# Two more triangular inverses on GpSimd, a weight preparation at another rank, and a planner with transfer lanes and re-measured durations

## The chip, the cores and the metric

The kernel runs on one core of a Trainium2 chip. The metric is the device time of one execution in microseconds (us). The core has five engines that run side by side, each with its own stream of instructions in a fixed order: TensorE (PE; its weight loads are PEld), VectorE (DVE), ScalarE (ACT), GpSimd (POOL) and SyncE (SP), which issues the DMA transfers. An instruction waits on semaphores until its inputs are there, and what stands behind it on its engine waits too.

## The reference

Three parts run one after the other: a recurrence over 768 steps for 4 batches of 8 heads, whose state is a 40x40 matrix for each head, and two feed-forward layers on the 3072 resulting rows of 320 values, with 2048 inner values each.

```
B, H, S, D = 4, 8, 768, 40
for t in range(S):
    y[:, :, t] = einsum('bhd,bhde->bhe', rt, state)
    Sa = einsum('bhde,bhe->bhd', state, at)
    state = state * wt[..., None, :] - einsum('bhd,bhe->bhde', Sa, bt) + einsum('bhd,bhe->bhde', vt, kt)
x = y.transpose(0, 2, 1, 3).reshape(B * S, H * D)
h = x @ w_in;  g = h * tanh(log1p(exp(h)));  x = g @ w_out      # layer 1
h = x @ w_in2; g = h * cos(h);               out = g @ w_out2    # layer 2
```

## The kernel before

The 32 heads are split into two halves of 16, and the 768 steps into 24 chunks of 32. A chunk of one half has a number g from 0 to 47, the two halves in turn; two successive numbers make a pair, bt = g // 2. Inside a chunk the recurrence is solved in closed form, for which a triangular 32x32 matrix must be inverted for every head. For each chunk these functions run:

- `pre(g)` prepares it. On VectorE: a running product of the decays (L571), its reciprocal (L576), a reverse scan (L577), and multiplies that make the operands AM (L585, two) and the keys KB (L591, two); on GpSimd two memsets of AM (L599). On TensorE the products between steps (L608, 8 matmuls for each bank, evicted in four pieces on VectorE, L618) and the transposed keys (L641). The part to be inverted is stored to DRAM (L631, L632).
- `inverse(bt)` loads both chunks of a pair into XM (L668), one matrix on each of 64 partitions, and inverts 16x16 blocks in 14 rounds of a multiply (L683) and an add (L681), then a memset of the diagonal (L690). Result stored (L694), loaded again in another layout as TT (L698). These 28 steps and the memset run on one engine: `own` says whether that is GpSimd or VectorE.
- `halves(bt)` joins the blocks to the 32x32 inverse: a transpose (L725) and one operation (L728) on VectorE, 32 small matmuls each of L720 and L722, a copy on ScalarE (L396).
- `chain(g)` is the recurrence proper. TensorE: L791, the product with the inverse (L805), L837, L863, L889, L933; VectorE: FR (L873), the next chunk's SV (L900), Y (L908). FR is loaded by L742 and L743, and the result is stored by L952.

Layer 1 runs on blocks of 256 rows: XR is loaded, ScalarE rounds it to XH (L1050), VectorE takes the rest XL (L1052), TensorE multiplies both with the split weights (h, L993), then the activation (L1066 to L1071) and the second product (o, L974). The first block needs the first four chunks of both halves. Layer 2 is like it (L1008, L1025), in blocks of 512. The weights are split into two parts by `prep`: ScalarE L465, VectorE L470 and L475, and a subtraction on GpSimd (L505). `prep` for layer 1 starts with the kernel, so it shares the engines with the first chunks.

Nothing of the order is left to a compiler. Every step is a `Task` with an engine, a duration, predecessors, and slots in rings of buffers (7 for PE, AM and FL, 3 for TT, 4 PSUM banks). `Plan.run` simulates the five engines with these numbers and always takes the task that can start first, by rank and priority (`prio`, lower is earlier); instructions are emitted in that order. TensorE's tasks have a column count (`cols`): where the count in a tick is under HOT, the planner doubles durations, and above DENSE it may keep matmuls of one tile shape together. A transfer is an SP task with a fixed latency, and it asks SP_SAFE us of spare time of a ring's buffer. Lines of `inverse` that the change touches:

```
own = bt >= 3
IE = G if own else V
t = P.add("POOL" if own else "DVE", 0.1 + 0.0022 * i * (15 - i) if own else 0.165, step(i, add), ...)
```

Of the kernel before, what the change touches and what calls it, by code (L numbers as in the profile page):

```python
# [20 lines left out]
S = 768  # L21
# [34 lines left out]
class Task:  # L56
    __slots__ = ("eng", "dur", "fn", "preds", "acq", "rel", "aset", "lat", "prio", "end", "n_wait", "succ", "ready", "cols", "engs", "takes", "name", "durs", "bias", "ffn", "port", "mode", "soft", "pull", "mate")

    def __init__(self, eng, dur, fn, preds=(), acq=(), rel=(), aset=None, lat=None, prio=0.0, cols=0.0, bias=BIAS, port=False):
# [16 lines left out]
        self.mate = None  # L76

# [3 lines left out]
DENSE = 4400.0  # L81
HOT = 2750.0
# [6 lines left out]
SP_SAFE = 1.0  # L89
# [9 lines left out]
class Plan:  # L99
# [23 lines left out]
    def run(self):  # L123
# [15 lines left out]
        tick, hot, count, tick_no = TICK, False, 0.0, 0  # L139
        order = {id(t): i for i, t in enumerate(self.tasks)}  # L140
        while done < len(self.tasks):
# [67 lines left out]
            if e == "PE":  # L209
# [20 lines left out]
            t.end = free[e] + (0.2 if t.lat is None else t.lat)  # L230
# [6 lines left out]
            for u in t.succ:  # L237
                for x in u.engs:
                    u.ready[x] = max(u.ready[x], free[e] + (HOP.get((e, x), 0.15) if t.lat is None else t.lat))
# [12 lines left out]
def body(ctx, tc, ins, out):  # L252
# [147 lines left out]
    def pa(key):  # L400
        return bank[P.at(key)]
# [22 lines left out]
    am_on, GLE = lambda g, d: ("DVE", 0.385), ("DVE",)  # L424
# [14 lines left out]
    def prep(layer, names, prio, after, stage, stage2, half):  # L439
# [5 lines left out]
        for kind, k, c0, n in jobs(layer):  # L445
# [32 lines left out]
            t3 = P.add("DVE", dve(n, 0.5), cvt1, preds=[t1], prio=prio, port=True)  # L478
# [75 lines left out]
    def pre(g):  # L554
# [38 lines left out]
        t_k = fifo("kb", P.add(*am_on(g, 0.65), kb_f(0), preds=[t_rp], acq=[("KB", k("KB"))], prio=pr, port=True))  # L593
        t_b = P.add(*am_on(g, 0.65), kb_f(1), preds=[t_k, t_a1], rel=[k("RP")] + ([] if g == 1 else [k("IN")]), prio=pr, port=True)
# [6 lines left out]
        t_z0 = P.add("POOL", 0.31, az_f(0), preds=[t_a1], prio=pr)  # L601
        t_z1 = P.add("POOL", 0.31, az_f(1), preds=[t_z0], prio=pr)
# [8 lines left out]
        t_g = P.add("PE", 0.46, g1, preds=[t_z1, t_b], acq=[("PA", k("G"), 4)], cols=925, prio=pr)  # L611
# [11 lines left out]
        for c2 in range(2):  # L623
            for p in range(2):
                t_gl.append(P.add("DVE", 0.27, gev(p, c2), preds=[t_g], rel=[k("G")], prio=pr))
# [17 lines left out]
        def kbe(e):  # L643
            def f(eng):
                kp = pa(k("KT"))[64 * e:64 * e + 64, 0:4 * QP].rearrange("r (q x) -> r q x", x=QP)
                for p in range(2):
# [4 lines left out]
                    cols=500, prio=pr)  # L651
        KBe[g] = [P.add(KBE, 0.4 + 0.2 * e, kbe(e), preds=[t_t], rel=[k("KT")], prio=pr) for e in range(2)]

    def inverse(bt):
# [17 lines left out]
        own = bt >= 3  # L672
# [684 lines left out]
```

## Time and profile before

| what | value |
|---|---|
| device time, median of 3 runs | 1081.68 us (1081.59 to 1082.09) |
| profiled execution, span from first to last instruction | 1089.5 us |
| TensorE busy in it | 1006.6 us (92%) |
| VectorE busy | 742.0 us (68%) |
| ScalarE busy | 544.0 us (50%) |
| GpSimd busy | 429.8 us (39%) |

The profiled execution is one execution with the hardware's recorder on, and its span is 7.8 us longer than the median of the timed runs. Durations are read from it, differences are applied to the median. An engine's busy time counts only its computing instructions. The clock column of the profile gives the TensorE clock that the chip granted, 1.00 being full speed.

### The profile page before, as it was taken

The page shows a single profiled execution, that of the slowest core. Times are in us where ns is not written, and L with a number is a line of the kernel's source. Part 1 is how long each engine was busy: PE and PEld are TensorE (multiplying, and loading weights), DVE is VectorE, ACT ScalarE, POOL GpSimd, SP SyncE. Part 2 cuts the span into 40 slices and gives each one's busy share as a digit, 9 for nine tenths or more (in the row PEclk, how much of TensorE's full clock was granted, in tenths as well). Part 3 has the DMA queues.
Part 4 walks back from the last instruction along what each step waited for, and adds up shares of the span by engine and source line. Part 5 has one row for each costly group of instructions (what it writes and reads, how often), then busy time and mean ns, then how long its engine had stood idle before and what let it go on. Part 6 is the DMA issues. An engine that isn't in the chain of part 4 may idle for free.

```text
span 1089.5 us, 36321 instructions
## 1 busy us (share of the span) xinstructions
PE 1006.6 (92%) x14888; PEld 926.8 (85%) x14888; DVE 742.0 (68%) x1652; ACT 544.0 (50%) x1338; POOL 429.8 (39%) x883
## 2 busy tenths in 40 slices
PE   1276899999999999999999999999999999999998
PEld 1265789888889988888998999999999999999997
DVE  8999888787577786678643797446655656565555
ACT  2345875655474655656564544434433434343433
POOL 4217646547344554355420242103333333333332
PEclk9999999999899999999999999999999999999999
DMA  6547665556445565455533543211100202010100
GB/s 206 149 134 231 173 166 145 154 143 170 108 137 160 145 168 127 122 152 151 137 90 100 173 152 96 85 42 35 42 13 1 54 1 54 1 40 1 25 1 25
DMA packets 109078, 111.88 MB, mean 103 GB/s; under 512 B 64112, under 2 KB 88688, under 8 KB 108912
## 3 DMA queue, kind: packets, MB, share of 16 engines
q1 hardware_dynamic: 108592, 109.24, 36.6%
q8 instruction: 117, 1.92, 0.7%
q14 instruction: 49, 0.40, 0.1%
q10 hardware_dynamic: 320, 0.33, 0.1%
HBM read 91.43 MB, written 18.09 MB: 101 GB/s over the span
## 4 chain that ended last, share of the span: by engine, by line
PE 75%; DVE 12%; DMA 5%; issue 4%; ACT 2%; SPq 1%; POOL 1%; DVEq 0%; POOLq 0%; ACTq 0%
PE bank L993 17%; PE bank L974 15%; PE bank L1008 14%; PE bank L1025 13%; PE bank L889 3%; PE bank L608 2%; DVE SV L900 2%; PE bank L863 1%; DMA VR<-in_vR_dram 1%; PE bank L641 1%; PE bank L837 1%; PE bank L791 1%; PE bank L933 1%; PE bank L805 1%; DVE AM L618 1%
## 5 line engine op out<-in xcount | busy, mean ns | idle before, releaser
L1154 POOL TENSOR_TENSOR GL<-H,GH 128x512 fp32r<-128x512 f32 x94 | 121.9, 1298 | 235.7 <-ACT GH L1152 219.1
L683 POOL TENSOR_TENSOR XT<-XM 64x14 f32<-64x14 f32 (+6 forms) x294 | 97.0, 330 | 174.5 <-DMA XM<-l_d 153.7
L396 ACT ACTIVATE FL<-bank 64x160 f32<-64x160 f32 (+1 forms) x375 | 101.4, 295 | 104.5 <-PE bank L641 51.6
L1145 ACT ACTIVATE T<-T,half_pi 128x512 f32<-128x512 f32 x96 | 69.5, 723 | 105.3 <-DVE T L1142 105.3
L1138 DVE TENSOR_SCALAR T<-bank 128x512 f32<-128x512 f32 x96 | 66.4, 692 | 76.7 <-PE bank L1008 63.2
L681 POOL TENSOR_TENSOR XM<-XM,XT 64x14 f32<-64x14 f32 (+6 forms) x294 | 106.0, 360 | 22.3
L1071 DVE TENSOR_TENSOR GL<-H,GH 128x512 fp32r<-128x512 f32 x96 | 70.1, 734 | 65.5 <-ACT GH L1068 63.7
L1147 DVE TENSOR_TENSOR H<-bank,T 128x512 f32<-128x512 f32 x96 | 66.1, 689 | 54.1 <-ACT T L1145 54.1
L1066 ACT ACTIVATE H<-bank 128x512 f32<-128x512 f32 x96 | 57.5, 598 | 87.9 <-PE bank L993 87.0
L1152 ACT ACTIVATE GH<-H 128x512 fp32r<-128x512 f32 x96 | 60.7, 632 | 73.9 <-DVE H L1147 73.9
L993 PE MATMUL bank<-XH,wih 128*128 128x256 f32 x448 | 95.4, 295 | 0.2 <-ACT GH L1068 0.2
L993 PE MATMUL bank<-XH,wil 128*128 128x256 f32 x448 | 89.7, 282 | 0.0
L993 PE MATMUL bank<-XL,wih 128*128 128x256 f32 x448 | 89.5, 282 | 0.0
L608 PE MATMUL bank<-AM,KB 104*64 104x64 f32 x768 | 37.0, 246 | 48.9 <-DVE KB L591 46.8
L618 DVE TENSOR_TENSOR AM<-bank,maskG 64x128 f32<-64x128 f32 x192 | 55.4, 288 | 35.8 <-PE bank L608 26.8
L608 PEld LDWEIGHTS bank<-AM,KB 104*64 104x64 f32 x768 | 30.5, 155 | 53.4 <-issue 35.4
L993 PEld LDWEIGHTS bank<-XH,wih 128*128 128x128 f32 x448 | 70.0, 192 | 2.2 <-ACT GH L1068 0.3
L993 PEld LDWEIGHTS bank<-XL,wih 128*128 128x128 f32 x448 | 69.7, 192 | 0.0
L993 PEld LDWEIGHTS bank<-XH,wil 128*128 128x128 f32 x448 | 69.6, 192 | 0.0
L1142 DVE SCALAR_TENSOR_TENSOR T<-T,bank 128x512 f32<-128x512 f32 x96 | 65.7, 685 | 2.4
L993 PE MATMUL bank<-XH,wix 128*128 128x256 f32 x224 | 67.1, 300 | 0.0
L900 DVE TENSOR_TENSOR SV<-bank,PE 40x160 f32<-40x160 f32 x184 | 58.9, 320 | 7.0 <-PE bank L889 3.8
(179 smaller groups left out, 2931.6 us busy)
## 6 DMA issues: line engine op xcount, KB each, us to landing
VR<-in_vR_dram SPq DMA_DIRECT2D x96, 160.0 KB
IN<-in_inT_dram SPq DMA_DIRECT2D x94, 161.4 KB
FR<-in_rI_dram SPq DMA_DIRECT2D x48, 180.0 KB
FR<-in_vF_dram SPq DMA_DIRECT2D x48, 144.0 KB
RA<-in_w_in_dram SPq DMA_DIRECT2D x12, 512.0 KB
RA<-in_w_out_dram SPq DMA_DIRECT2D x10, 512.0 KB
SV<-in_vS_dram SPq DMA_DIRECT2D x96, 52.0 KB
TMP<-in_w_in_dram SPq DMA_DIRECT2D x9, 512.0 KB
```

The lines of the kernel that those rows point to most:

```text
L396: A.activation(o, i, AF.Copy)
L608: PE.matmul(gp[c0:c0 + 64, q // 2], kb()[:, q].rearrange("p a t -> p (a t)"), am()[0:104, :, q], start=True, stop=True)
L681: IE.tensor_tensor(out=b[:, 0:i, i + 1:16], in0=b[:, 0:i, i + 1:16], in1=tv, op=ALU.add)
L683: IE.tensor_tensor(out=tv, in0=bc(b[:, i:i + 1, i + 1:16], (2 * n, i, w)), in1=bc(b[:, 0:i, i:i + 1], (2 * n, i, w)), op=ALU.mult)
L900: V.tensor_tensor(out=svn[r, p, :, 64 * h:64 * h + D], in0=fp[r, :, C:], in1=bc(pev(h)[r, :, C:C + 1], (40, 4, D)), op=ALU.mult)
L974: PE.matmul(o, l[:, f, tsl], r, start=(first and f == 0 and i == 0), stop=(last and f == 1 and i == 2))
L993: PE.matmul(hp[:, f], pss[i][0], pss[i][1], start=(i == 0), stop=(i == 7))
L1008: PE.matmul(bank[P.at((key, "h"))][:, 0:512], pss[i][0], pss[i][1], start=(i == 0), stop=(i == 7))
L1025: PE.matmul(o, l, r, start=(ft == 0 and i == 0), stop=(ft == NFF - 1 and i == 2))
L1071: gl = P.add(GLE, (dve(512),), lambda eng, Hv=Hv, key=key: EN[eng].tensor_tensor(out=GL_t[P.at((key, "gl"))], in0=Hv(), in1=GH_t[P.at((key ...
L1145: c = P.add("ACT", act(512, False, 1), lambda f=f, Tv=Tv: A.activation(Tv(f), Tv(f), AF.Sin, scale=-TWO_PI, bias=half_pi), preds=[b], aset ...
L1154: gl = P.add(*((VG, (pool(512), dve(512))) if final and quad == 7 else ("POOL", pool(512))), lambda eng, f=f, Hv=Hv, key=key: EN[eng].tens ...
```

## The change

`own` becomes true from the second pair on: the inverses of the pairs bt = 1 and bt = 2 go to GpSimd too; that of bt = 0 stays on VectorE. The preparation of layer 1's weights goes from priority -4921 to -4941, so it ranks ahead of two chunks' more tasks. The rest changes the planner only: SP's transfers go through a model with eight lanes, each with its own size and latency, in place of a fixed latency; TensorE's instruction fetching is modelled in blocks of 256; durations, column counts and the two column thresholds are replaced; SP_SAFE becomes 0. No instruction but those of the two inverses changes its engine by an edit of its own. The new numbers also give every engine another order. Lines behind L134 move by 17 to 36 (L683 becomes L719, L805 becomes L841, L993 becomes L1029).

```
-SP_SAFE = 1.0
+SP_SAFE = 0.0
-DENSE = 4400.0
-HOT = 2750.0
+DENSE = 5240.0
+HOT = 3277.0
+ISSUE, GAP_I, LANES, LAND = 0.36, 0.06, 8, 0.15
+DMAS = {"pre.ld": ((0.85, 1.65), (0.75, 1.65)), "inverse.st": ((0.2, 1.1), (0.2, 1.1)),
...
+BLOCK, AHEAD_C, FETCH = 256, 78, 3.5
...
+            if t.dm:
+                cur = st
+                for size, l0 in t.dm:
+                    cur = max(cur, lanes[nd % LANES]) + ISSUE
+                    srv = max(srv, cur + l0) + size
+                    lanes[nd % LANES], nd = srv, nd + 1
+                    cur += GAP_I
+                dur = cur - st
...
+            t.end = srv + LAND if t.dm else free[e] + (0.2 if t.lat is None else t.lat)
...
-    am_on, GLE = lambda g, d: ("DVE", 0.385), ("DVE",)
+    am_on, GLE = lambda g, d: ("DVE", 0.43), ("DVE",)
...
-        own = bt >= 3
+        own = bt >= 1
...
-                t = P.add("POOL" if own else "DVE", 0.1 + 0.0022 * i * (15 - i) if own else 0.165, step(i, add), preds=[t], lat=0.1 if own else 0.04, prio=pr, port=True)
+                t = P.add("POOL" if own else "DVE", 0.1 + 0.0022 * i * (15 - i) if own else 0.22, step(i, add), preds=[t], lat=0.1 if own else 0.04, prio=pr, port=True)
...
-                t = P.add("PE", 0.48, mm, preds=list(preds) + [t], cols=880, acq=[("PH", (key, "h"))] if first else [],
+                t = P.add("PE", 0.48, mm, preds=list(preds) + [t], cols=1024, acq=[("PH", (key, "h"))] if first else [],
...
-    S_V = P.add("DVE", 2.0, setup_v, prio=-9e5)
+    S_V = P.add("DVE", 4.0, setup_v, prio=-9e5)
...
-    wr1 = prep(1, ("w_in", "w_out"), -4921.0, [W1_AFTER()], ("RW", "H"), ("RL", "RA1"), half1)
+    wr1 = prep(1, ("w_in", "w_out"), -4941.0, [W1_AFTER()], ("RW", "H"), ("RL", "RA1"), half1)
```

In the rows of the order below, a row is a line, an operation, and its output and inputs with their tile. A number behind a name tells which buffer of a ring it is; TT_233 to TT_235 are the inverses of three successive pairs in turn.

VectorE, before, where the second pair's inverse begins (XM and XT are the inverse, PE, RP, AM and KB a chunk's preparation):

```order
L576 RECIPROCAL D1R<-PE_200 104x8
L577 SCALAR_TENSOR_TENSOR RP_217<-IN_195,D1R 104x264
L585 TENSOR_TENSOR AM_207<-IN_195,PE_200 40x256
L591 TENSOR_TENSOR KB_219<-IN_195,RP_217 104x8x32
L585 TENSOR_TENSOR AM_207<-IN_195,PE_200 40x256
L683 TENSOR_TENSOR XT<-XM 64x14
L591 TENSOR_TENSOR KB_219<-IN_195,RP_217 104x8x32
L681 TENSOR_TENSOR XM<-XM,XT 64x14
L571 SCALAR_TENSOR_TENSOR PE_201<-IN_194,D_193 104x264
L683 TENSOR_TENSOR XT<-XM 64x26
L576 RECIPROCAL D1R<-PE_201 104x8
L577 SCALAR_TENSOR_TENSOR RP_217<-IN_194,D1R 104x264
```

The same chunks' preparation on VectorE in the new order:

```order
L607 SCALAR_TENSOR_TENSOR PE_200<-IN_195,D_193 104x264
L726 MEMSET XM 64x16
L511 SCALAR_TENSOR_TENSOR H_179<-TMP,H_179 128x512
L612 RECIPROCAL D1R<-PE_200 104x8
L613 SCALAR_TENSOR_TENSOR RP_217<-IN_195,D1R 104x264
L621 TENSOR_TENSOR AM_207<-IN_195,PE_200 40x256
L627 TENSOR_TENSOR KB_219<-IN_195,RP_217 104x8x32
L621 TENSOR_TENSOR AM_207<-IN_195,PE_200 40x256
L607 SCALAR_TENSOR_TENSOR PE_201<-IN_194,D_193 104x264
L627 TENSOR_TENSOR KB_219<-IN_195,RP_217 104x8x32
```

Steps of an inverse stood between the multiplies; now the memset that ends the first pair's is the last of them here, and the two chunks' preparation stands together.

TensorE, before, up to the first feed-forward matmul (L993; TT_235 is pair three's inverse, RS the right-hand sides that it is multiplied with):

```order
L720 MATMUL bank_146<-TA,TT_235 32x32 x32
L722 MATMUL bank_146<-TT_235,TB 32x16 x32
L805 MATMUL bank_145<-RS_236,TT_235 32x40 x16
L805 MATMUL bank_147<-RS_237,TT_235 32x40 x16
L837 MATMUL bank_144<-ident,ZS_232 40x128 x4
L993 MATMUL bank_148<-XH_187,wih_164 128x256 x2
```

The same place in the new order (TT_233 is pair four's inverse, L841 the product with it, L1029 the first feed-forward matmul):

```order
L644 MATMUL bank_147<-AM_206,KB_219 64x64 x8
L841 MATMUL bank_145<-RS_236,TT_233 32x40 x16
L841 MATMUL bank_144<-RS_237,TT_233 32x40 x16
L677 MATMUL bank_146<-ident,KB_219 128x104 x4
L873 MATMUL bank_147<-ident,ZS_232 40x128 x4
L644 MATMUL bank_145<-AM_207,KB_219 64x64 x8
L899 MATMUL bank_146<-VR_224 64x64 x8
L873 MATMUL bank_147<-ident,ZS_232 40x128 x4
L1029 MATMUL bank_148<-XH_187,wih_164 128x256 x2
```

The first feed-forward matmul stood behind the products with pair three's inverse; now it stands behind those with pair four's, and six more small groups follow the first of them.

GpSimd, before, ahead of its first inverse, which is pair four's (L505 is a weight subtraction, L599 the memset of AM):

```order
L599 MEMSET AM_203 64x256 x2
L505 TENSOR_TENSOR wil_165<-H_180,wih_164 128x512
L505 TENSOR_TENSOR wix_166<-H_181,wix_166 64x512
L599 MEMSET AM_204 64x256 x2
L505 TENSOR_TENSOR wol1a<-H_179,woh1a 128x512
L683 TENSOR_TENSOR XT<-XM 64x14
L681 TENSOR_TENSOR XM<-XM,XT 64x14
L683 TENSOR_TENSOR XT<-XM 64x26
```

GpSimd, in the new order, ahead of its first inverse, which is pair two's:

```order
L541 TENSOR_TENSOR wil_165<-H_180,wih_164 128x512
L541 TENSOR_TENSOR wix_166<-H_181,wix_166 64x512
L635 MEMSET AM_207 64x256 x2
L719 TENSOR_TENSOR XT<-XM 64x14
L717 TENSOR_TENSOR XM<-XM,XT 64x14
L719 TENSOR_TENSOR XT<-XM 64x26
L717 TENSOR_TENSOR XM<-XM,XT 64x2x13
```

The first inverse on GpSimd came when the memsets had gone once round AM's ring of seven (AM_203 to AM_209) and on to AM_204; now it comes in the first round, at AM_207, and ahead of the first subtraction of the second weight matrix (wol1a).

## Rows read from the trace of the kernel before

**Rows 1.** Busy by stretch: stretch, us; PE PEld DVE ACT POOL (instructions); clock, DMA, GB/s.

```profile
0.00:115.00 115.00, 55.73 (x1325) 47.24 (x1326) 105.29 (x303) 47.19 (x133) 42.84 (x102) 1.00 0.62 177
115.00:150.00 35.00, 31.06 (x750) 27.95 (x749) 30.14 (x72) 28.85 (x73) 18.05 (x39) 1.00 0.64 180
150.00:200.00 50.00, 49.06 (x929) 44.91 (x928) 41.23 (x108) 32.01 (x95) 35.94 (x87) 1.00 0.54 146
200.00:600.00 400.00, 386.19 (x8772) 351.04 (x8771) 270.86 (x715) 228.60 (x684) 176.23 (x540) 0.98 0.52 138
600.00:1089.50 489.50, 484.61 (x3121) 455.71 (x3119) 294.48 (x457) 207.35 (x356) 156.77 (x116) 1.00 0.16 46
```

**Rows 2.** TensorE's waits up to 115 us: line, releaser: us, times, longest.

```profile
PE bank L608 <- DVE KB L591: 44.4, 8, 17.0
```

**Rows 3.** Order of time around the first feed-forward matmul: start, us, engine, line, operation.

```profile
113.78 0.95 DVE L1052 TENSOR_TENSOR XL<-XR,XH 128x768 fp32r<-128x768 f32 x1
114.73 0.78 PE L993 MATMUL bank<-XH,wih 128*128 128x256 f32 x2
```

**Rows 4.** Order of time: L889 early and later, [idle before].

```profile
95.08 2.19 PE L889 MATMUL bank<-FR,FL 104*64 104x72 f32 x32
...
139.62 1.22 PE L889 MATMUL bank<-FR,FL 104*64 104x72 f32 x32 [0.96 <-DVE FR L873]
```

**Rows 5.** Lines of VectorE up to 160 us: instructions, busy us, mean ns, idle before.

```profile
L683 DVE TENSOR_TENSOR XT<-XM 64x14 f32<-64x14 f32 (+6 forms) x42 | 9.4, 224 | 0.8
L681 DVE TENSOR_TENSOR XM<-XM,XT 64x14 f32<-64x14 f32 (+6 forms) x42 | 8.1, 193 | 0.9
```

**Rows 6.** Order of time: first and last steps of pair two's and pair four's inverse.

```profile
47.93 0.17 DVE L683 TENSOR_TENSOR XT<-XM 64x14 f32<-64x14 f32 x1
...
71.82 0.07 DVE L690 MEMSET XM<- 64x16 f32 x1
...
89.90 0.21 POOL L683 TENSOR_TENSOR XT<-XM 64x14 f32<-64x14 f32 x1 [3.65 <-DMA XM<-l_d]
...
102.72 0.12 POOL L690 MEMSET XM<- 64x16 f32 x1
```

**Rows 7.** The page's costliest groups: the multiplies of the inverses on GpSimd.

```profile
L683 POOL TENSOR_TENSOR XT<-XM 64x14 f32<-64x14 f32 (+6 forms) x294 | 97.0, 330 | 174.5 <-DMA XM<-l_d 153.7
```

**Rows 8.** Lines of VectorE by form, up to 160 us: the chunks' work.

```profile
L585 DVE TENSOR_TENSOR AM<-IN,PE 40x256 f32<-40x256 f32 x28 | 17.7, 631 | 0.3
...
L900 DVE TENSOR_TENSOR SV<-bank,PE 40x160 f32<-40x160 f32 x32 | 10.3, 321 | 1.4 <-PE bank L889 0.8
...
L908 DVE TENSOR_TENSOR Y<-bank,PE 104x128 f32<-104x128 f32 x16 | 4.6, 289 | 0.3
...
L576 DVE RECIPROCAL D1R<-PE 104x8 f32<-104x8 f32 x15 | 3.0, 201 | 0.2
```

**Rows 9.** Order of time on VectorE and GpSimd, 99 to 105 us.

```profile
99.21 0.85 POOL L681 TENSOR_TENSOR XM<-XM,XT 64x36 f32<-64x36 f32 x1
...
101.86 0.41 DVE L591 TENSOR_TENSOR KB<-IN,RP 104x256 f32<-104x256 f32 x1
...
102.93 1.57 POOL L505 TENSOR_TENSOR wol1a<-H,woh1a 128x512 fp32r<-128x512 f32 x1
103.36 1.42 DVE L591 TENSOR_TENSOR KB<-IN,RP 104x256 f32<-104x256 f32 x1
```

**Rows 10.** Order of time: pair three's inverse stored, and its product.

```profile
98.65 0.95 SPq L694 DMA_DIRECT2D t_d<-XM  x2
...
112.82 1.29 PE L805 MATMUL bank<-RS,TT 32*32 32x40 f32 x64 [1.06 <-ACT TT L396]
```

**Rows 11.** Lines of TensorE by form, 200 to 560 us: the chunks' work.

```profile
L889 PE MATMUL bank<-FR,FL 104*64 104x72 f32 x1024 | 38.2, 229 | 0.0
...
L720 PE MATMUL bank<-TA,TT 16*32 16x32 f32 x1088 | 13.0, 194 | 1.6 <-DVE D1R L576 1.1 <-issue 0.5
```

**Rows 12.** TensorE's waits, 115 to 600 us, the largest one of issue.

```profile
PE bank L722 <- issue: 3.0, 4, 1.7
```

More of the change, by code (lines that the diff above doesn't have):

```diff
@@ L76, in __init__ @@
         self.mate = None
+        self.code = 64 if self.name == "chain.ztm" and dur < 0.4 else CODE.get(self.name, 8)
+        self.dm = DMAS.get(self.name) if eng == "SP" else None
+        if self.dm and "prep" in self.name and dur < 0.5:
+            self.dm = ((1.05, 1.3),)
 TIE = 97
 TICK = 10.24 / 3
-DENSE = 4400.0
-HOT = 2750.0
+DENSE = 5240.0
+HOT = 3277.0
 MODE = {"pre.g1": "128x64", "chain.rvz": "128x64", "chain.fmm.f": "128x64", "chain.rhs": "128x32",
@@ L88 @@
 WAIT = 8.0
-SP_SAFE = 1.0
+SP_SAFE = 0.0
+ISSUE, GAP_I, LANES, LAND = 0.36, 0.06, 8, 0.15
+DMAS = {"pre.ld": ((0.85, 1.65), (0.75, 1.65)), "pre.ldm": ((0.2, 1.0), (0.2, 1.0)), "inverse.ld": ((0.25, 1.2), (0.25, 1.2)),
+        "inverse.st": ((0.2, 1.1), (0.2, 1.1)), "inverse.<lambda>": ((0.5, 1.5),),
+        "load_step.f1": ((0.95, 1.65), (0.5, 1.65)), "load_step.f2": ((0.9, 1.5), (0.9, 1.5)),
+        "load_step.f3": ((0.2, 1.2), (0.2, 1.2)), "prep.<lambda>": ((2.15, 1.4),), "chain.yst": ((0.37, 1.25), (0.37, 1.25)),
+        "layer1.ld": ((0.8, 1.4), (0.25, 1.3), (0.25, 1.3)), "layer1.<lambda>": ((0.4, 1.05),),
+        "layer2.ld": ((0.3, 1.3),) * 4, "layer2.store": ((0.27, 1.3),) * 2}
+CODE = {"pre.g1": 32, "early.uu": 64, "early.<lambda>": 64, "halves.mm.f": 128, "chain.rhs": 64, "chain.zmm": 64,
+        "chain.rvz": 32, "chain.fmm.f": 32, "chain.sel": 20, "outs.mm": 6, "outs_wide.mm": 6}
+BLOCK, AHEAD_C, FETCH = 256, 78, 3.5
 def mode_cost(a, b):
@@ L225, in run @@
                     count += t.cols
-                recent.append((st + dur, t.cols))
+                at, per = st, dur / t.code
+                for i in range(code, code + t.code):
+                    if i % BLOCK == 0 and i // BLOCK in fetched:
+                        w = max(0.0, fetched[i // BLOCK] - at)
+                        at, dur = at + w, dur + w
+                        self.starved += w
+                    if (i + AHEAD_C) % BLOCK == 0:
+                        b = (i + AHEAD_C) // BLOCK + 1
+                        fetched[b] = max(at, fetched.get(b - 1, 0.0) - FETCH / 2) + FETCH
+                    at += per
+                code += t.code
+                recent.append((st + dur, t.cols))
+            if t.dm:
[6 more added lines that the diff above has]
+                dur = cur - st
             free[e] = st + dur + sw
@@ L238, in run @@
                 for x in u.engs:
-                    u.ready[x] = max(u.ready[x], free[e] + (HOP.get((e, x), 0.15) if t.lat is None else t.lat))
+                    u.ready[x] = max(u.ready[x], t.end if t.dm else free[e] + (HOP.get((e, x), 0.15) if t.lat is None else t.lat))
                 u.n_wait -= 1
@@ L878, in chain @@
         for h in range(2):
-            ve[h] = P.add("DVE", 0.41, rve(h), preds=[r0] + z[2 * h:2 * h + 2] + [ve[i] for i in range(h)], rel=[k("V")], prio=pr)
+            ve[h] = P.add("DVE", 0.43, rve(h), preds=[r0] + z[2 * h:2 * h + 2] + [ve[i] for i in range(h)], rel=[k("V")], prio=pr)
         yb, yc = divmod(c, 2)
@@ L919, in chain @@
             if not last:
-                s = [P.add("DVE", 0.315, sev(h, p), preds=[ft, io[nx][2]], prio=pr) for p in range(2)]
+                s = [P.add("DVE", 0.34, sev(h, p), preds=[ft, io[nx][2]], prio=pr) for p in range(2)]
             sevs += s
```

54 lines of the change are left out of this document (28 added, 26 removed).

## The prediction

> **What bounds the kernel now.** I read the table by stretches first, then the waits of TensorE, then the order of time around the first feed-forward matmul. TensorE is busy in 1006.6 of the 1089.5 us (the five stretches added) [rows 1]. That work is the same before and after, so what can move is its 82.9 us of idle time. 59.3 of them lie ahead of 115, 3.9 from 115 to 150, 0.9 to 200, 13.8 from 200 to 600 and 4.9 behind. So the start is the stage to read. There VectorE is busy 105.3 of 115 us, ScalarE 47, GpSimd 43, and TensorE's one large wait is for the keys that VectorE makes, 44.4 us in 8 waits, the longest 17.0 [rows 2]. VectorE works at XL from 113.78, the last input of layer 1's first block, and the first feed-forward matmul starts at 114.73 [rows 3]. From there TensorE has layer 1 to fill itself with, and it is never idle for long. The start is VectorE's, the rest is TensorE's.
>
> A second thing is lost in the start. The same 32 matmuls of L889 take 2.19 us at 95.08 and 1.22 at 139.62 [rows 4], though the granted clock reads 1.00 in both stretches [rows 1]. So what a step at the start is worth is counted at the price that it would have later, since that is where it would otherwise stand.
>
> **The inverses leave VectorE.** One inverse is 28 multiply and add steps and a memset. VectorE ran 84 of these steps, three pairs of chunks, in 9.4 + 8.1 us [rows 5], so 5.85 us a pair; two pairs leave it, **11.7 us**. The steps were strewn between other work: those of the second pair took from 47.93 to 71.82, 23.9 us, while the fourth pair's on GpSimd took from 89.90 to 102.72, 12.9 us [rows 6], with other work in between. So a step is slower on GpSimd (330 ns in the mean [rows 7] against 208) and the inverse is through sooner after its start. GpSimd has room: 42.8 us busy of 115 [rows 1], about 69 with two more inverses.
>
> **What fills VectorE instead.** The order has the same 15 weight tiles prepared ahead of XL as before, but more of the attention. Preparation of chunks gains 18 instructions of six lines (two L571, L576 and L577, four L585, two L591, four L618; L585 is the largest group at 631 ns and L576 the smallest at 201 [rows 8]), 8.1 us by their means. The recurrence gains eight L900 (321 ns, the largest group), four L873 and four L908 (289 ns, the smallest) [rows 8], 5.4 us. One transpose and one L728 add 0.9. In go 14.4, out 11.7: **+2.7 us**, and XL moves from 113.8 to 116.5. If some 3.5 of VectorE's 9.7 us of gaps [rows 1] closed as well, it would come at 113; that is the lower end.
>
> **What else the first matmul waits for.** In TensorE's order both products with the inverse of pair three stood ahead of the first feed-forward matmul (L805); now those of pair four stand there too, and pair four's inverse is the third in a row on GpSimd. Pair two can start near 44. Three inverses at 12.9, four weight subtractions among them that GpSimd did not have there before, 1.57 us at most [rows 9], and the memsets of the keys, 7.5 in all: 90 if GpSimd never waits. If pair four waits for its chunks' preparation, which stands some 74 us of work deep on VectorE, its transfer ends near 82 and its inverse at 95 (estimates, from the order and the means by line). The way from there is read from pair three: store issued at 98.65, product at 112.82 [rows 10], 14.2 us, so 104 to 109. Then come six small groups of TensorE, 7 us at the slow rate: 111 to 116. SP's queue can add to that. In the new order the store of an inverse stands behind loads of FR that wait for TensorE and VectorE, and the loads behind it wait too. One such wait of 6 us makes it 122. By VectorE the first matmul comes at 117.4, by this path at 111 to 122. I take **118**, 3.3 us later than now, nearer VectorE's row because that one is counted and the path has slack at several places.
>
> **What TensorE has done by then.** Ahead of its first feed-forward matmul the order now holds 16 more of L608, 4 of L641, 32 each of L791, L805, L720 and L722, 24 of L863, 32 of L889, 16 of L933 and 12 of L837: one pair of chunks, give or take a step. From 200 to 560 these ten lines take 187 us for 32 chunks (L889 the largest with 38.2, L720 the smallest with 13.0 [rows 11]), 11.7 a pair, and 11.0 without the overlap at the seams. That work no longer stands between 118 and the end. Gain: 11.0 - 3.3 = **7.7 us**. By the lower end (first matmul at 114) it is 11.7, by the upper (122) 3.7.
>
> **Everything else that moves.** The planner's numbers (durations, columns, eight transfers in flight, fetched instructions) emit nothing; they reorder. Behind the start I cost that at nothing, since TensorE is busy 386 of 400 us there [rows 1] with feed-forward work that can be drawn ahead of a wait. Where the cover fails the row is issue, in which nothing visible is waited for, 3.0 us in the largest of four lines and 7.6 in all [rows 12]. The new plan can win perhaps 5 of it, or lose as much, since it has 106 changes of tile shape among the small matmuls against 93. Bounds -5 and +5, taken as 0. Layer 2's order is the same but for a few neighbours.
>
> **Locks between VectorE and GpSimd.** A multiply of VectorE took 1.42 us at 103.36, and its like 0.41 at 101.86; a 1.57 us GpSimd subtraction had started at 102.93 [rows 9]. So the one engine can hold up the other. The 56 steps moved to GpSimd can each do this: from nothing to 56 x 0.33 = 18 us of VectorE, and half a step each is 9.2. I leave it at nothing in the sum: the 0.41 at 101.86 lies within the fourth pair's inverse [rows 6, 9], and the three others of its kind in there took no longer, 0.40 to 0.42. Both ends stay for the range. The Trainium skill (SBUF — State Buffer, Who interferes with whom) says that a VectorE instruction with two SBUF inputs contends with a GpSimd instruction that reads SBUF, and that the second waits for the whole of the first. By that rule the trace agrees at 103.36, and the rule speaks against this change: it is what gives the first rival its chance.
>
> **The rivals.** (a) The locks take it back: 9.2 us on top of 116.5, the first matmul at 126.6, 11.9 late, gain 11.0 - 11.9: 1082 to 1083. With locks a little shorter it is 1081. For it: VectorE stays as full and GpSimd is fuller. Against: the multiplies beside pair four's inverse did not stretch. (b) The chain of inverses sets the start, and the kernel ends **slower**. TensorE takes its instructions in order, so nothing passes a product that waits for T. If each inverse is stretched by 3 us, as single steps are beside VectorE (one took 0.85 us at 99.21 [rows 9] against the mean of 0.33), and SP holds one store for 6 us, the first matmul starts at 109 + 7 + 9 + 6 = 131, 16.3 late: 5.3 lost, 1087. It decides from 126 on, where the delay passes the 11.0. For it: the order leaves no feed-forward work ahead of the product. Against: pair four's chunks are prepared early and little else stands between the inverses. (c) The start gains as forecast and the issue waits go too: 7.7 + 5, so 1069. (d) The change does not do what it says: the new numbers fit the chip no better than the old, and behind the start the plan returns the gain in waits of TensorE from 118 to 200, where there were 4.8 us. Within 2 us of now; it shares (a)'s time.
>
> **How the numbers follow.** The profiled execution's span is 1089.5 us and the median of the runs 1081.68, 7.8 less; differences are taken from the median. 1081.68 - 7.7 = **1074**. Chances: forecast, 1070 to 1079, 0.55; (c) 0.13; (a) and (d) together 0.16; (b) 0.16. The 8-in-10 range leaves out a tenth on each side: 1065 below (gain 11.7 and the five of issue) and 1086 above, within (b). About 0.2%, 2.2 us, is what a measurement of this kernel can tell from no change. Faster takes the forecast and (c), 0.68; same is most of (a) and (d), 0.15; slower is (b) and the worst of (a), 0.17.
>
> **What would show it.** In the profile after, no XM or XT steps on VectorE behind some 45 us, and 56 more on GpSimd. The first L1029 matmul (now L993) at 116 to 121. TensorE's idle time ahead of the first one at most 62 us though it comes later. VectorE about 90% busy up to there. Ahead of 114, VectorE's count was too high; behind 125, its last wait tells why: a product waiting for T of pair four is (b), XL waiting behind multiplies of VectorE that last 0.6 us and more beside XM steps is (a). If the first matmul comes at 118 and the end moves by less than 4 us, my assumption of nothing behind the start is what failed.

## The result: slower, where faster was forecast

The changed kernel takes 1.0055 times the time of the kernel before, 95% interval 1.0032 to 1.0078: medians of 1091.26 us and 1082.62 us over 17 executions each. The forecast was 1074, and the range ended at 1086. On a second chip the ratio was 1.0081 (1.0049 to 1.0113). Single executions of one kernel lie far apart, 1081.8 to 1096.8 us for the changed kernel and 1080.2 to 1092.2 for the one before, so single profiles are compared by parts and verdicts come from the ratios.

That spread also corrects how the profile of before was read. Its span of 1089.5 us was not 7.8 us of recorder on top of 1081.68. In the changed kernel the profiled execution is one of the timed ones, 1088.50 us with a span of 1086.8, 1.7 apart. So the profile of before showed one of its longer executions, about 1091 us.

Of the changed kernel, first the busy time by stretch. The columns are those of [rows 1].

```profile
0.00:115.00 115.00, 64.06 (x1612) 54.69 (x1612) 98.48 (x261) 51.02 (x147) 66.64 (x173) 0.92 0.63 183
115.00:150.00 35.00, 31.29 (x467) 28.08 (x468) 30.39 (x75) 28.48 (x71) 21.80 (x37) 0.84 0.77 214
150.00:200.00 50.00, 48.97 (x1082) 45.15 (x1080) 36.82 (x94) 30.07 (x87) 26.70 (x76) 1.00 0.46 124
200.00:600.00 400.00, 383.65 (x8636) 347.40 (x8636) 267.51 (x711) 228.26 (x682) 173.54 (x542) 0.98 0.51 139
600.00:1086.80 486.80, 481.96 (x3096) 452.99 (x3095) 293.48 (x457) 206.87 (x354) 158.23 (x116) 1.00 0.15 45
```

Against [rows 1], GpSimd went from 42.8 to 66.6 us ahead of 115, as the two inverses said it would, and TensorE did 64.1 us there instead of 55.7. But VectorE, 105.3 before, is busy only 98.5 us of the 115. TensorE's waits up to 130 us (against [rows 2]):

```profile
PE bank L644 <- DVE KB L627: 25.5, 5, 16.6
PE bank L644 <- POOL XM L717: 12.5, 1, 12.5
```

The second row names a new releaser, a step of an inverse on GpSimd, but only in name: the matmul that waited started at 45.9, it reads AM and the keys KB and no XM, and VectorE had finished those keys at 45.8. So the two rows together, 38.0 us, are, as far as the order shows, the wait on VectorE that was 44.4 before.

Then the order of time around the first feed-forward matmul (against [rows 3]), start, us, engine, line:

```profile
107.65 0.83 ACT L1086 ACTIVATE XH<-XR 128x768 fp32r<-128x768 f32 x1
...
124.17 0.93 DVE L1088 TENSOR_TENSOR XL<-XR,XH 128x768 fp32r<-128x768 f32 x1
...
125.58 0.78 PE L1029 MATMUL bank<-XH,wih 128*128 128x256 f32 x2
```

The first feed-forward matmul comes at 125.6, not 118. Its rounded input XH was started at 107.7, earlier than before (111.1), but XL came 16.5 us after XH, where it came 2.7 us after it before. XL was done at 125.1, and TensorE's own queue came to the matmul at 125.6.

Layer 2 takes 300.3 to 300.6 us from its first weight load on in every profile of this study but one (land_late, 301.7). So all that differs lies ahead of it. I split that part four ways: the start of the first feed-forward matmul (in the tables the start of its weight load, up to 0.1 us earlier); TensorE's idle time from there to layer 2; half of the time that it spent there at the lower clock, as an estimate of what the clock cost; and the rest, which is work at full rate. The idle time is the stretch less TensorE's busy time. The clock is that of the trace's record, in which 0.50 is 1.2 GHz; for the time ahead of the record's first entry the matmuls' own durations give the level.

| profile | first matmul | idle | at half clock | rest | start + rest |
|---|---|---|---|---|---|
| before, first profile | 114.7 | 19.2 | 16.8 | 646.8 | 761.5 |
| before_again | 115.9 | 17.5 | 10.6 | 646.6 | 762.5 |
| changed, first profile | 125.5 | 18.2 | 14.6 | 635.1 | 760.6 |
| after_again | 124.2 | 24.7 | 38.1 | 634.8 | 759.0 |

The rest fell by 11.7 us: the chain work done early, forecast at 11.0, is there. The first matmul came 8 to 11 us later, forecast at 3.3. So the start gains 1 to 3.5 us instead of 7.7. And behind it the changed kernel loses 3 us more in idle time, in the mean of two profiles each, and 6 us more by the clock (half of 26.4 - 13.7). These three come to some +7 us, in line with the ratios.

### The profile page after: what moved, and what is told of

It is laid out like the page before. It is cut to its first block, busy times and chain, and to the rows that moved or that the text cites. A ratio compares the mean times of both kernels' runs of the same rounds, so it can differ in the third digit from the quotient of the medians.

```text
span 1086.8 us, 36354 instructions
## 1 busy us (share of the span) xinstructions
PE 1009.9 (93%) x14888; PEld 928.3 (85%) x14888; DVE 726.7 (67%) x1593; ACT 544.7 (50%) x1339; POOL 446.9 (41%) x941
## 5 line engine op out<-in xcount | busy, mean ns | idle before, releaser
L719 POOL TENSOR_TENSOR XT<-XM 64x14 f32<-64x14 f32 (+6 forms) x322 | 113.3, 352 | 201.1 <-DMA XM<-l_d 178.3
L432 ACT ACTIVATE FL<-bank 64x160 f32<-64x160 f32 (+1 forms) x375 | 101.2, 295 | 97.1 <-PE bank L677 48.7
L717 POOL TENSOR_TENSOR XM<-XM,XT 64x14 f32<-64x14 f32 (+6 forms) x322 | 110.3, 343 | 24.6
L1029 PE MATMUL bank<-XH,wih 128*128 128x256 f32 x448 | 95.3, 295 | 1.0 <-ACT GH L1104 0.6
L1029 PE MATMUL bank<-XH,wil 128*128 128x256 f32 x448 | 89.6, 282 | 0.0
L1029 PE MATMUL bank<-XL,wih 128*128 128x256 f32 x448 | 89.3, 281 | 0.0
L1029 PEld LDWEIGHTS bank<-XH,wih 128*128 128x128 f32 x448 | 70.0, 192 | 3.8 <-ACT GH L1104 1.4
L1029 PEld LDWEIGHTS bank<-XL,wih 128*128 128x128 f32 x448 | 69.4, 191 | 1.9 <-issue 1.9
L1029 PEld LDWEIGHTS bank<-XH,wil 128*128 128x128 f32 x448 | 69.5, 192 | 0.0
L1029 PE MATMUL bank<-XH,wix 128*128 128x256 f32 x224 | 67.3, 300 | 1.8 <-issue 1.8
L936 DVE TENSOR_TENSOR SV<-bank,PE 40x160 f32<-40x160 f32 x184 | 59.0, 320 | 13.6 <-PE bank L925 10.8
L644 PEld LDWEIGHTS bank<-AM,KB 104*64 104x64 f32 x768 | 31.2, 158 | 42.5 <-issue 27.8
```

What stands on the lines that cost most here:

```text
L432: A.activation(o, i, AF.Copy)
L644: PE.matmul(gp[c0:c0 + 64, q // 2], kb()[:, q].rearrange("p a t -> p (a t)"), am()[0:104, :, q], start=True, stop=True)
L717: IE.tensor_tensor(out=b[:, 0:i, i + 1:16], in0=b[:, 0:i, i + 1:16], in1=tv, op=ALU.add)
L719: IE.tensor_tensor(out=tv, in0=bc(b[:, i:i + 1, i + 1:16], (2 * n, i, w)), in1=bc(b[:, 0:i, i:i + 1], (2 * n, i, w)), op=ALU.mult)
L1029: PE.matmul(hp[:, f], pss[i][0], pss[i][1], start=(i == 0), stop=(i == 7))
```

## The experiments

All ratios are against the kernel before on the same chip, with 95% intervals. Each run's column "TT" is VectorE's wait on the load of an inverse (TA from TT) from 130 to 780 us; that view turned out to tell kernels planned with the change's transfer lanes from those without. "Idle" and "at half clock" are TensorE's, from its first feed-forward matmul to layer 2. Each run is one order of the instructions, so a ratio tells of that order.

| run | ratio | interval | first matmul | TT | idle | at half clock |
|---|---|---|---|---|---|---|
| before_again | 0.9982 | 0.9961 to 1.0004 | 115.9 | 4.7 | 17.5 | 10.6 |
| before_tie | 1.0034 | 1.0005 to 1.0062 | 129.1 | 9.6 | 18.2 | 26.5 |
| before_tie42 | 0.9953 | 0.9930 to 0.9976 | 114.9 | 14.0 | 11.6 | 17.4 |
| before_tie29 | 1.0042 | 1.0009 to 1.0075 | 115.8 | 14.1 | 16.0 | 11.5 |
| own_only | 1.0083 | 1.0052 to 1.0113 | 110.9 | 8.3 | 27.9 | 42.5 |
| no_lanes | 1.0039 | 1.0007 to 1.0070 | 122.4 | 8.7 | 16.3 | 15.2 |
| no_lanes_tie18 | 0.9987 | 0.9959 to 1.0015 | 123.3 | 11.0 | 14.7 | 11.8 |
| after_again | 1.0081 | 1.0049 to 1.0113 | 124.2 | 38.8 | 24.7 | 38.1 |
| after_tie9 | 1.0140 | 1.0101 to 1.0178 | 126.7 | 34.4 | 22.0 | 25.7 |
| after_tie18 | 1.0234 | 1.0191 to 1.0277 | 124.8 | 37.1 | 35.0 | 53.1 |
| plan_only | 1.0222 | 1.0179 to 1.0264 | 125.2 | 23.8 | 26.1 | 34.2 |
| lanes_only | 1.0204 | 1.0165 to 1.0243 | 125.2 | 29.2 | 27.9 | 21.4 |
| first_xl | 1.0220 | 1.0145 to 1.0294 | 108.2 | 24.2 | 34.2 | 60.6 |
| old_cols | 1.0182 | 1.0127 to 1.0236 | 124.5 | 26.6 | 31.6 | 37.2 |
| tt_late | 0.9948 | 0.9924 to 0.9971 | 112.6 | 8.0 | 17.7 | 14.8 |
| tt_late_tie18 | 1.0222 | 1.0179 to 1.0265 | 112.0 | 27.0 | 36.9 | 56.2 |
| land_late | 1.0003 | 0.9983 to 1.0023 | 125.7 | 7.1 | 10.4 | 2.7 |
| land_late_tie18 | 1.0118 | 1.0073 to 1.0164 | 131.2 | 16.4 | 16.8 | 27.7 |

The first profiles had 8.6 us of TT waits in the kernel before and 34.4 in the changed one.

### Both kernels again, and each half of the change alone

before_again and after_again are the two kernels without an edit.

> The kernel before, once more, for a second profile. Theory 1 (the start decides: what is gained is lost again by the later first feed-forward matmul): first L993 within 1 us of 114.7 again, span as the time, and a profile of a typical execution (about 1082) differs from the first one (1091) by fewer or shorter stretches at half clock behind 200 us. Rival (the executions differ by waits, not by the clock): same stretches at half clock, and 8 us fewer idle time of TensorE.

> The changed kernel once more. Theory 1: first L1029 within 1 us of 125.6 again; median 1086 to 1093; executions as far apart as before (1082 to 1096), by the stretches at half clock. Rival: the first L1029 itself comes at another time in another execution, by 3 us or more.

The first matmul repeats within 1.3 us, a little over the 1 us of the first theory and under the 3 us of its rival, so the start is the order's and not chance. The clock behind it is what varies: 14.6 us at half clock in one execution of the changed kernel, 38.1 in the next, with 6.5 us more idle time. The theory of the start alone falls here: it leaves 1 to 3.5 us of gain, and the kernel is slower.

own_only is the kernel before with

```
-        own = bt >= 3
+        own = bt >= 1
```

and plan_only is the changed kernel with that line put back.

> The kernel before with the inverses of pairs two and three on GpSimd alone, under the old numbers of the planner. If the inverses on GpSimd are what costs (GpSimd's queue delays the products): first L993 at 122 or later, time 1086 to 1092. If the new numbers cost it: first L993 at 112 to 118, time 1076 to 1083.

> The changed kernel with pairs two and three back on VectorE, the new numbers kept. If the inverses on GpSimd cost it: 1078 to 1084. If the new numbers cost it: 1086 to 1092, and the first L1029 is no later than in the kernel before, so that the loss shows behind 200 us.

Both runs fell outside their cases in part: own_only's loss is that of its first case, but its first matmul fits neither; plan_only lost more than twice what its second case said, with a later first matmul (125.2) that no case had. Under the old numbers the first matmul came at 110.9, earlier, and the kernel was still slower by 0.8%: TensorE was idle for 13.3 us between 110.9 and 200, where the kernel before has 4.9 from 115 to 200. With the inverses back on VectorE the new numbers cost 2.2%, far more than the whole change. So in these orders the larger loss comes with the planner's numbers, and so does the late first matmul.

### Single parts of the planner, and XL's place

first_xl ranks the first block's input ahead of the chunks' work:

```
-                   acq=[("XH", (xk, "xh"))], prio=pr0)
+                   acq=[("XH", (xk, "xh"))], prio=pr0 if blk else -1e4)
...
-            preds=[th], acq=[("XL", (xk, "xl"))], rel=[(xk, "xr")], prio=pr0, port=True)
+            preds=[th], acq=[("XL", (xk, "xl"))], rel=[(xk, "xr")], prio=pr0 if blk else -1e4, port=True)
```

> The changed kernel with XH and XL of layer 1's first block ranked ahead of the chunks' work, nothing else edited. In the changed kernel XH is there at 108 and XL comes at 124 on VectorE. If XL's place on VectorE is what makes the first feed-forward matmul late: it starts at 108 to 113, and the time is 5 to 10 us under that of the changed kernel. If it only moves work about (chain work that was done early now stands behind it): it starts as early and the time stays within 3 us of the changed kernel. If TensorE's product with pair four's inverse is the cause: it stays at 120 or later.

The matmul started at 108.2 as its first case says, and the time rose by 1.4% over the changed kernel, which no case said. So an early first matmul is not enough by itself: here less chain work lies ahead of it, and TensorE's idle time behind it grew to 34.2 us. It is one order; tt_late below is early too, at 112.6, and fast.

The planner gives each duration a deviation of at most 1%, drawn from the number `TIE` (97 in both kernels), so another number gives another order of the same instructions. before_tie is the kernel before with `TIE = 98`. old_cols has the old column counts (h 880, o 840 and the others), `DENSE = 4400.0` and `HOT = 2750.0` in the changed kernel. no_lanes has `self.dm = None` and `SP_SAFE = 1.0` in it.

> The kernel before with another number for breaking ties (each duration of the planner gets another deviation of at most 1%), nothing else. If a change of order alone, with no meaning in it, moves the time: more than 0.4% away from the kernel before, and other stretches at half clock behind 200 us; its order has the first L993 at row 111 of TensorE in place of 92, so 119 to 125 us. If the order is of little weight: within 0.3%.

> The changed kernel with the old column counts and the old two thresholds of the planner. If the new counts make TensorE fall to half clock more often: stretches at half clock behind 200 us under 14 us in the profile, and time 4 us or more under that of the changed kernel. If they don't: within 3 us of it.

> The changed kernel with transfers planned as before (one fixed latency, SP_SAFE 1). If the eight lanes cost it (the order trusts transfers that come later): idle time of TensorE from its first feed-forward matmul to layer 2 down from 18 to 25 us by 4 or more, and time 4 us or more under that of the changed kernel. If they help or are neutral: as the changed kernel or slower.

A tie number without meaning moved the first matmul from 115 to 129 and the time by 0.34%, between its two cases: not nothing, and less than the changes above. Old counts did not help. Without the lanes the ratio was 1.0039, better than 1.0055 and 1.0081, but its interval overlaps both of theirs, so this run alone settles nothing.

### Is it a draw of the order?

Any changed number gives another order, so I drew more orders of both kernels by the tie number, choosing numbers for which the planner's own total was as low as it is for the two kernels (1065.5 to 1066.8 us): `TIE = 18` and `TIE = 9` in the changed kernel, `TIE = 42` and `TIE = 29` in the one before.

> The changed kernel with another number for breaking ties (deviations of at most 1% in the planner's durations), one for which the planner's own total is 1065.5 us, against 1066.8 with the number it has. If the change's place of loss is its meaning (first feed-forward matmul late, waits behind the start): 1.004 to 1.012 times the kernel before, first L1029 at 122 to 127. If it is a draw of the order: anywhere from 0.997 to 1.02.

> As the run before it, with a third number (planner's total 1066.0 us). Meaning: 1.004 to 1.012, near the other two. Draw: apart from them by more than 0.6%.

> The kernel before with another number for breaking ties, planner's total 1065.6 us against 1066.4. Its first L993 stands at row 92 of TensorE as in the kernel before. If the kernel before is a lucky draw: 1.004 or more. If the old numbers with the old places of the inverses are better by their meaning: 0.997 to 1.003.

> As the run before it, with another number (planner's total 1065.7 us; first L993 at row 92). Lucky draw: 1.004 or more. Meaning: 0.997 to 1.003.

The cases point both ways: 1.0234 lies past both ranges and 1.0140 meets the case of a draw; 0.9953 lies under both ranges and 1.0042 meets the case of a lucky draw. So the order alone matters: draws of one kernel differ by up to 1.8%, and the planner's total does not see it. But meaning is there too: the kernel before draws 0.995 to 1.004 in four orders, the changed one 1.006 to 1.023 in three, and the two sets do not overlap, though their nearest members, 1.0042 and 1.0055, lie within each other's intervals. Here the view of VectorE's waits from 130 to 780 us told them apart. Columns: who waits, releaser, us in all, times, longest. The kernel before, in before_again:

```profile
DVE TA L725 <- DMA TT<-t_d: 4.7, 2, 4.3
```

The changed kernel, in after_again:

```profile
DVE TA L761 <- DMA TT<-t_d: 38.8, 15, 6.5
```

The changed kernel with tie 18:

```profile
DVE TA L761 <- DMA TT<-t_d: 37.1, 16, 5.1
```

At that point the seven profiles planned with lanes had 24 to 39 us of this wait, and the seven without had 5 to 14. Among the seven with lanes it does not rank the times: 34.4 us go with 1.0055 and 23.8 with 1.0222. The planner's table shows where the wait comes from. For the load of an inverse it counts 0.36 + 1.5 + 0.5 + 0.15 = 2.5 us, where it counted 0.5 + 3.0 before. In after_again the fifteen transposes that waited started 2.4 to 6.0 us after their load's issue, thirteen of them later than 2.5. Of the 38.8 us, 30.4 lie behind the load's issue; in the other 8.4 it was not yet issued. The two transfers ahead of it, the load of XM and the store of L730, count 2.4 and 2.2 us by the same table, where they counted 4.0 before; first steps on GpSimd that waited for XM started 2.5 to 6.8 us after its issue in that profile, where the table has 2.4. So VectorE reaches the transpose ahead of the data, and what stands behind it waits: FR, SV and Y, which TensorE needs. The order of time on VectorE in after_again shows one such stop, with [idle before <- releaser]; 1.9 of its 5.4 us lie ahead of the load's issue at 417.86, which came 3.2 us after that of the store whose result it reads:

```profile
414.73 1.21 DVE L654 TENSOR_TENSOR AM<-bank,maskG 64x128 f32<-64x128 f32 x4 [0.86 <-PE bank L644]
421.30 0.45 DVE L761 STREAM_TRANSPOSE TA<-TT 128x256 f32<-128x256 f32 x1 [5.36 <-DMA TT<-t_d]
422.16 1.65 DVE L909 TENSOR_TENSOR FR<-bank,maskR 64x256 f32<-64x256 f32 x4 [0.42 <-ACT GH L1104]
```

The Trainium skill (DMA: Bandwidth & Descriptors, Latency and other measured facts) gives an HBM access latency of 0.2 us in the mean and 2 us at high load. By that a landing could move by some 1.8 us (an estimate, the difference of the page's two figures); the trace agrees in direction, but 2.4 to 6.0 us is a spread of 3.6, twice that.

### The lanes, tested

lanes_only puts the lanes and `SP_SAFE = 0.0` on the kernel before and nothing else that acts (the code for instruction fetching comes along, but its fetch times are fixed at 3.5 us from the plan's start); no_lanes_tie18 is no_lanes with `TIE = 18`. tt_late is the changed kernel with one number edited, tt_late_tie18 the same with `TIE = 18`:

```
-        "inverse.st": ((0.2, 1.1), (0.2, 1.1)), "inverse.<lambda>": ((0.5, 1.5),),
+        "inverse.st": ((0.2, 1.1), (0.2, 1.1)), "inverse.<lambda>": ((0.5, 4.0),),
```

> The kernel before with the planner's eight lanes and SP_SAFE 0 alone: its inverses stay where they were, and its durations, column counts, thresholds and weight rank too. If the lanes are the cause by themselves: 1.008 or more, with 24 us or more of VectorE's waits on TT from 130 to 780 us (the kernel before: 8.6). If they only cost together with three inverses on GpSimd: within 0.4% of the kernel before.

> The changed kernel without the lanes and with SP_SAFE 1, tie number 18; with lanes that number had 1.023. Lanes as the cause: 1.008 or less. A draw of the order: as likely over as under 1.015.

> The changed kernel; in the planner's table of transfers the load of an inverse (TT) alone is taken to land 2.5 us later (base 1.5 becomes 4.0). If VectorE's transposes come up ahead of the landed inverse, and that is what TensorE waits for behind the start: VectorE's waits on TT from 130 to 780 us fall from 34 to 39 us to under 18, TensorE's waits on the transpose to under 2, and the time to 1.002 or less of the kernel before. If lanes cost it in another way (order of SP, other loads): waits on TT fall and the time stays at 1.006 or more.

> The same edit on the changed kernel with the tie number 18, which had 1.023. Inverse loads as the cause: 1.010 or less. Another cause in the lanes: 1.015 or more.

The lanes alone, with the inverses where they were, cost 2.0%. Taken from the slowest draw they give back 2.5%, to 0.9987. lanes_only, no_lanes_tie18 and tt_late each met the case of the lanes or of the inverse load as the cause. VectorE's waits on TT, in lanes_only:

```profile
DVE TA L761 <- DMA TT<-t_d: 29.2, 16, 7.0
```

in no_lanes_tie18:

```profile
DVE TA L761 <- DMA TT<-t_d: 11.0, 6, 4.7
```

and in tt_late:

```profile
DVE TA L761 <- DMA TT<-t_d: 8.0, 4, 5.3
```

So the lanes, with the SP_SAFE that goes with them, cost time: the seven kernels planned with them stand at 1.006 to 1.023, the seven without at 0.995 to 1.008. That is shown over the orders drawn. For the changed kernel's own order taking them out is not enough to show it (1.0039 against 1.0055 and 1.0081), and own_only, at 1.0083 without them, shows that another order can cost as much. One number for the inverse load makes the changed kernel faster than both kernels, 0.9948 times the kernel before. On tie 18 it did nothing for the time (1.0222, the case of another cause in the lanes): 27.0 us of the wait were left, 8.8 of them in one stop. So it is not the inverse load alone. The last two runs move every landing by 1.5 us, in the changed kernel and with `TIE = 18`:

```
-ISSUE, GAP_I, LANES, LAND = 0.36, 0.06, 8, 0.15
+ISSUE, GAP_I, LANES, LAND = 0.36, 0.06, 8, 1.65
```

> The changed kernel; every transfer is taken by the planner to land 1.5 us later (LAND 0.15 becomes 1.65), the lanes and all else kept. If the lanes cost because they take transfers to land too early: VectorE's waits on TT from 130 to 780 us under 18 and 1.002 or less of the kernel before. If the queueing or SP_SAFE 0 is what costs: 1.006 or more, with waits on TT still over 24.

> The same on tie number 18, for which a later TT alone did not help (1.022, 27 us of waits on TT, of which 8.8 behind one load of XM that came late). Landing of all transfers as the cause: 1.006 or less. Queueing or SP_SAFE: 1.012 or more.

The first met its case (1.0003, 7.1 us). The second fell from 1.0234 to 1.0118, half of the way and on neither side of its bounds. So later landings gave back all of the loss in one order and half of it in the other. Each edit also draws a new order, and 1.0118 lies within what the lanes' draws gave, so that early landings are the larger part of what the lanes cost is likely and not shown. What the rest is, SP_SAFE, the lanes' queueing or the draw, stays open; SP_SAFE was never changed alone. Whether the TT wait is itself the loss or a mark of an order that trusts early landings in many places is open too: TensorE's own waits name TA for only 2 to 9 us of it. What ranks the kernels better is all of TensorE's waits on VectorE from 130 to 780 us, added up: 7.4 and 13.1 us in the changed kernel's two profiles and 12.6 to 21.4 in the six others with lanes, 2.8 to 10.8 in the eight without; 2.5 in tt_late, 4.2 and 6.6 in the two runs with late landings; and 18.0 in tt_late_tie18, which is as slow as its number was before. So much of the loss seems to reach TensorE through VectorE, by more steps than the transpose alone.

## Why the prediction was wrong, step by step

**What bounds the kernel, and that the start is VectorE's.** Right as read from one profile, but that was one of the longer executions, and its 13.8 us of idle time from 200 to 600 was taken as a floor that could only move by 5.

**The inverses on GpSimd.** Right in size. First and last steps of pairs two and four there, and the way of pair four's to TensorE (against [rows 6, 10]):

```profile
44.13 0.24 POOL L719 TENSOR_TENSOR XT<-XM 64x14 f32<-64x14 f32 x1 [7.93 <-DMA XM<-l_d]
...
59.29 0.12 POOL L726 MEMSET XM<- 64x16 f32 x1
...
80.62 0.21 POOL L719 TENSOR_TENSOR XT<-XM 64x14 f32<-64x14 f32 x1 [2.06 <-DMA XM<-l_d]
...
93.20 0.12 POOL L726 MEMSET XM<- 64x16 f32 x1
...
97.17 0.78 SPq L730 DMA_DIRECT2D t_d<-XM  x2
...
117.31 1.29 PE L841 MATMUL bank<-RS,TT 32*32 32x40 f32 x64
```

Pair two started at 44 and pair four ended at 93.3, forecast 90 to 95 (the memsets in that sum are those of AM, not of the keys). SP issued the store 3.9 us later, which the sum had allowed for with 6. The way from store to product took 20.1 us in place of 14.2, so the product came at 117.3, past the 104 to 109 of the sum and 2 us past the 115 that the allowance of 6 on top makes of it. But it did not wait for the inverse: the copy that completes TT (L432 on ScalarE) ended at 113.4, and TensorE came to the product 3.9 us later, straight from other matmuls. By the prediction's own sign that speaks against rival (b).

**VectorE's count, and the locks.** Up to the first matmul VectorE was busy 107.5 us against 105.2, +2.3 where +2.7 was counted. So locks cost VectorE nothing that shows in this sum, and rival (a) falls by its own mechanism. The rule of the Trainium skill that speaks for it (SBUF — State Buffer, Who interferes with whom) is not refuted, but these 56 steps did not bring it to bear on VectorE's time.

**The failed term of the start** is in "XL moves from 113.8 to 116.5": it adds the +2.7 us of work and leaves VectorE's gaps as they were, or closes some. They grew from 9.5 to 18.0 us up to the first matmul, and XL came at 124.2. Its largest waits in the changed kernel up to 125.5 us are for ScalarE, TensorE and a transfer:

```profile
DVE H L506 <- ACT H L501: 2.9, 2, 1.7
DVE SV L936 <- PE bank L925: 2.7, 3, 1.5
DVE TA L761 <- DMA TT<-t_d: 1.9, 3, 1.0
DVE AM L654 <- PE bank L644: 1.8, 2, 1.5
```

before, the largest wait of this kind up to the first matmul was one of 0.7 us in all. 2.3 of work and 8.5 of gaps are the 10.8 us by which the matmul came later. TensorE's own last wait ahead of it is for VectorE too:

```profile
122.98 1.12 PE L644 MATMUL bank<-AM,KB 104*64 104x64 f32 x16 [1.50 <-DVE KB L627]
```

My reading is that an engine relieved of independent work has less to put between dependent steps. The gaps fit it: 15.7 to 26.4 us in the thirteen profiles with these inverses on GpSimd, 9.5 to 14.5 in six of the seven with them on VectorE, but 16.4 in the seventh, lanes_only. A late matmul does not follow from it alone: own_only has gaps of 17.5 us and starts at 110.9, while plan_only and lanes_only start at 125.2 with no inverse moved. What the order puts ahead of XL decides as well.

**What TensorE has done by then.** Right: 11.7 us in the row "rest", forecast 11.0. The later first matmul took it back, as rival (b) put it ("decides from 126 on"), at 125.6 and not at its 131. That rival gives 1082 at this point, so it doesn't carry the result.

**The step that failed most** is "Everything else that moves", costed at nothing with bounds of 5 us either way. The argument was that feed-forward work covers behind 200 us. The runs show 3 us more idle time and 6 us more by the clock there, in the mean of two profiles each; the start's shortfall against 7.7 is 4 to 7 us. TensorE's waits on VectorE from 130 to 780 us were 8.1 and 6.5 us before and are 7.4 and 13.1 now, so feed-forward work does not always cover what VectorE's queue holds up, and the falls of the clock cost more than the waits. Rival (d), that the new numbers fit the chip no better, is what happened, with the wrong place (118 to 200 us, where the changed kernel had no more idle time than before) and the wrong price (nothing, where lanes alone cost 2.0%). Issue waits, on which the bounds rested, hardly moved: 7.7 us from 130 to 780 against 7.6.

**What the inverses are worth alone** stays unsettled. With old numbers own_only gave 1.0083; without lanes, 1.0039 and 0.9987; in tt_late 0.9948, where start and rest together are 753.4 us against 761.5 and 762.5 before, 8 to 9 us gained and close to the 7.7 of the forecast. before_tie42 reached 0.9953 with no inverse moved. So one order shows such a gain, and it is no larger than a draw of the order; that the inverses made it is not shown.

## What to carry to other kernels

In an order that is fixed ahead of time, a transfer's duration that fits the earliest landings of a trace is not yet a safe one (2.5 us here, where those waited for took 2.4 to 6.0): an in-order engine that arrives early at a transfer holds up all that stands behind it, while one that arrives late loses only its own slack. I would plan transfers by their late landings, and I would read the waits on transfers of every engine after a change of such numbers, not only the idle time of the one that is busiest. And before a change of under 1% is credited to its idea, draw its order and that of the old kernel a few times; here draws alone gave 0.995 to 1.004 and 1.006 to 1.023.

## What the runs showed of the hardware

**Short waits cost twice.** In after_again TensorE waited 1.41 us on issue and 1.36 us on VectorE, with little but small matmuls between, and then ran at half clock for 17 us. From the order of time on TensorE:

```profile
434.96 0.61 PE L841 MATMUL bank<-RS,TT 32*32 32x40 f32 x42 [1.41 <-issue]
...
440.27 0.75 PE L756 MATMUL bank<-TA,TT 16*32 16x32 f32 x64 [1.36 <-DVE AM L654]
...
443.11 2.13 PE L925 MATMUL bank<-FR,FL 104*64 104x72 f32 x32
```

and by stretch, the clock being the third number from the end:

```profile
430.00:442.00 12.00, 9.23 (x273) 8.09 (x271) 8.40 (x20) 8.26 (x26) 0.00 (x0) 1.00 0.60 158
442.20:459.20 17.00, 17.00 (x236) 15.27 (x236) 11.07 (x29) 5.48 (x15) 9.40 (x32) 0.50 0.46 132
460.00:475.00 15.00, 15.00 (x329) 13.44 (x321) 9.68 (x30) 9.92 (x33) 0.42 (x2) 1.00 0.44 123
```

TensorE was busy in all of the 17 us. If at 1.2 GHz it did half of what it could have, 8.5 us were lost behind 2.8 of waits; the 32 matmuls of L925 took 2.13 us here and 1.22 at full rate (L889 before) [rows 4], less than twice, so the loss was somewhat smaller. Every such fall between 135 us and layer 2, in nineteen profiles (the twentieth, land_late, has none), had 0.6 to 3.8 us of idle time of TensorE in the 5 us ahead of it. The Trainium skill (TensorE: Matmul & The Clock Gate, HAM oscillation — how this bites in real kernels) describes waits for transfers that send TensorE back to its lower clock. The trace agrees that waits do it, though these two, 1.41 and 1.36 us, were for issue and for VectorE. The same wait did not always do it. In the first profile of the changed kernel, which has the same order, L756 came late behind the same step of VectorE, without a wait on issue ahead of it, and no fall followed:

```profile
437.56 0.78 PE L756 MATMUL bank<-TA,TT 16*32 16x32 f32 x64 [2.15 <-DVE AM L654]
```

Such falls are most of the difference between the two executions of each kernel that were profiled: half of the difference at half clock is 11.8 of the 16.5 us between the spans of the changed kernel, and 3.1 of 3.8 before.

**A clock of 1.00 can mean that nothing was recorded yet.** The table showed 1.00 for the first 115 us of the kernel before [rows 1], with matmuls at half rate [rows 4]. In before_again the record starts earlier and has the level:

```profile
96.00:119.00 23.00, 13.43 (x322) 11.65 (x320) 18.24 (x38) 11.57 (x33) 14.07 (x26) 0.50 0.75 209
120.00:140.00 20.00, 17.46 (x478) 15.47 (x476) 19.21 (x44) 16.05 (x42) 12.46 (x31) 1.00 0.54 156
```

So the start runs mostly at 1.2 GHz until feed-forward work comes, in the kernel before as in the changed one. Not all of it: in the changed kernel's first profile the record has 1.00 from 88.9 to 92.3 and from 106.0 to 109.4, and 16 matmuls of L899 took 0.69 us at 106.57 against 1.12 at 102.61.
